# Attention with the two heads of a pair side by side in the array, splits on all partitions, one output instruction for both heads

## The chip, the core and the metric

The program runs on one core of a Trainium2 chip. TensorE (PE) multiplies matrices and writes PSUM; its weight loads have a row of their own in the profile (PEld). VectorE (DVE), ScalarE (ACT) and GpSimd (POOL) do the elementwise work, and SyncE (SP) issues the DMAs. Each engine takes its own instructions in the order in which they stand, and semaphores hold the engines together. The metric is the device time of one execution in microseconds (us).

## The reference, cut to what matters

```python
def _attn_ref(q, k, v):                       # (4, 8, 576, 64) each, float32
    q_rot, k_rot = (rotate(q), rotate(k))     # x * cos + (halves swapped, signed) * sin
    scores = (1 / np.sqrt(64)) * np.matmul(q_rot, k_rot.transpose(0, 1, 3, 2))
    attn = np.exp(scores - np.max(scores, axis=-1, keepdims=True))
    attn = attn / (np.sum(attn, axis=-1, keepdims=True) + 1e-09)
    return np.matmul(attn, v)
# the heads joined: x (4, 576, 512); then
# xk, xr: x mixed with x one token earlier, by mu_k and mu_r
# k = relu(xk @ w_k);  x = sigmoid(xr @ w_r) * (k * k @ w_v)
# u = x + token mix (576 -> 256 -> 576);  out = u + relu(u @ w_ch1) @ w_ch2
```

## The kernel before

The 32 heads are taken as 16 pairs, A and B. A pair's scores are worked on in nine tiles of 128 query rows (`TILES`, line 29): A0 to A3, B0 to B3, and R, which holds the last 64 rows of A and of B. To keep float32 accuracy every factor is split into a high part and the rest. After the rotation (`rope`, on POOL), `split_hi` (ACT) and `split_lo` (DVE for q, POOL for k) work on one head at a time, so on 64 partitions: `kst` holds a head's k with the high part on its own 64 partitions and the rest on the other 64, and `qst` holds q with the high part on all 128 and then the rest on all 128, for which a DMA copies it across (line 307). A tile of scores is then 4 matmuls over 128 partitions (2 splits of q by 2 halves of 288 keys; R takes 8), `emit_S`, line 384, into one of two buffers of PSUM (`S_p`).

Of each tile DVE takes the row maximum (`emit_max`), ACT the exponential with its sum (`emit_exp`), DVE the factor 1/sum (`emit_den`, `emit_rc`), ACT the high half of p in float16 (`emit_hi`), DVE the low half (`emit_lo`), and a DMA transposes both (`emit_tr`). A pair's output is made in four units, one head and 256 or 320 queries each (`emit_pv`, line 457): 9 matmuls of a 128-column stationary operand that holds the high and the low half of that head's v side by side. The two halves of the result are added by an ACT copy (line 465) and a DVE instruction (line 474) on 64 partitions.

`a_step` is one tile's turn, and `prep` places what the next pair needs. During the first 4 pairs the weights of the next layer are converted on DVE (`Conv`, line 163). From pair 4 on, `a_step` also draws from `kvr_gen`: the matmuls with w_k (`kp`, line 628) and w_v (`vp`, line 646) of the batches whose attention is done. These are plain float32, and the chip runs each as two instructions. `PRI` sets priorities and a scheduler makes the fixed order of each engine from them; the w_k and w_v work has the lowest one. `v_row` (line 318, a one-column stationary operand) and `v_all` (line 339, a one-row one) make the scale of v. After the attention come the weights of the later layers, the last w_k tasks and the two mixing layers, which the change does not touch.

Of the kernel before, what the change touches and what calls it, by code (L numbers as in the profile page):

```python
# [18 lines left out]
NP = H // 2  # L19
# [18 lines left out]
BUFS = dict(raw=6, vr=2, v16=2, e=7, p16=3, pt0=1, pt1=2, tm=2, sm=4, sc=3, la=1, lf=1, xs=4, xk=6, t=2, q=2, vt=2, wd=3)  # L38
# [25 lines left out]
def body(tc, qk, vw, tabs, ident, mu, w_k, w_v, w_r, w_t1, w_t2, w_c1, w_c2, out):  # L64
# [41 lines left out]
    with ctx:  # L106
# [130 lines left out]
        raw_p = right("raw", BUFS["raw"])  # L237
        tab_p = right("tab", 1)
        st_p = right("st", 1)
# [4 lines left out]
        pt0_p = right("pt0", BUFS["pt0"])  # L244
        pt1_p = right("pt1", BUFS["pt1"])
        tm_p = right("tm", BUFS["tm"])
# [3 lines left out]
        tab = tab_p.tile([128, 2, S], F32, name="tab")  # L250

        raw_t, v_t, v16_t, sc_t = {}, {}, {}, {}

        kst = [st_p.tile([128, S], F32R, name=f"kst{x}") for x in range(2)]
        qst = [st_p.tile([128, 2, QW], F32R, name=f"qst{x}") for x in range(2)]
        NG = B * NP

        @prio("ld")
        def ld_raw(g, ab=((0, 1), (1, 1), (0, 0), (1, 0))):
            if g >= NG:  # L260
                return
            for j, k in ab:
                t = raw_p.tile([128, S], F32, tag="raw", name="raw")
                sp.dma_start(t, qk[g // NP, g % NP, :, j, k])
                raw_t.setdefault(g, [[None] * 2 for _ in range(2)])[j][k] = t
# [9 lines left out]
        @prio("rope")  # L275
        def rope(g, j, k, e):
            t = raw_t[g][j]
            if k < 2:
                o = tt(e, t[k], t[k], tab[:, k], ALU.mult)
# [68 lines left out]
        @prio("v16")  # L348
        def v_hi(g):
            t = v16_p.tile([128, 9, 4, 64], F16, tag="v16", name="v16")  # L350
            v16_t[g] = t
            copy("A", v_t[g], v_t[g], sc_t[g][:, 0:1])
            act.activation(out=t[:, 0:5, 0::3, :], in_=v_t[g].rearrange("p c (h d) -> p c h d", h=2), func=AF.Copy)

        @prio("v16")
        def v_lo(g):
            v, t = v_t[g], v16_t[g]
            for x in range(2):
                o, hi = t[:, 0:5, 1 + x, :], t[:, 0:5, 3 * x, :]
                tt("P", o, v[:, :, 64 * x:64 * x + 64], hi, ALU.subtract)  # L360

        @prio("v16")
        def v_shift(g):
            t = v16_t[g]
# [5 lines left out]

        @prio("S")
# [624 lines left out]
```

## Time and profile before

| what | value |
|---|---|
| median of 3 runs | 1046.34 us (1046.04 to 1047.02) |
| the profiled execution | 1049.78 us, span 1048.0 us, mean granted clock 0.951 |
| busy, share of the span | PE 86%, weight loads 75%, DVE 61%, ACT 50%, POOL 36% |
| first matmul of scores of pair 0 | about 20 us |
| last matmul of scores of pair 15 | about 523 us |
| DMA over the span | 130.48 MB, of 216365 packets 175712 under 512 B |

The first two rows differ because the profiled execution is another one. The shares are means over very different stretches: until 149 us attention runs beside the conversion of weights, until 523 us beside the w_k and w_v matmuls, and after that there is no attention.

### The profile page before, as it was taken

How to read it: one execution, taken by the hardware profiler on the slowest of the kernel's cores; microseconds unless marked ns; L12 is line 12 of the kernel's file. 1: busy time of each engine (PE TensorE's matmuls, PEld its weight loads, DVE VectorE, ACT ScalarE, POOL GpSimd, SP SyncE). 2: the span in 40 equal slices, each digit the busy share in tenths (PEclk: the TensorE clock that was granted, in tenths of full speed). 3: DMA queues.
4: the chain of work that ended last, by engine and by line, in shares of the span. 5: the costliest groups of instructions: out<-in, count | busy, mean ns of one | idle time of the engine just before them, and what ended most of it. 6: DMA issues, size and time to landing. Idle time of an engine off the chain costs nothing.

```text
span 1048.0 us, 15540 instructions
## 1 busy us (share of the span) xinstructions
PE 903.7 (86%) x5488; PEld 782.1 (75%) x5488; DVE 643.4 (61%) x1283; ACT 525.4 (50%) x1114; POOL 377.3 (36%) x344
## 2 busy tenths in 40 slices
PE   2447557989889997799948899999999999999998
PEld 1335344767667776578827789899999999999997
DVE  6999999877678778878689636953323312231111
ACT  3666667767667786778656353443233112211110
POOL 6653476553355544532035513461132012201010
PEclk9986667999999999899979999999999999999999
DMA  6899989997888888987792044311020002000000
GB/s 195 217 206 229 220 194 181 176 203 167 182 166 190 190 177 161 198 185 157 133 321 98 23 137 159 134 42 28 1 91 24 23 2 75 1 24 1 24 23 23
DMA packets 216365, 130.48 MB, mean 125 GB/s; under 512 B 175712, under 2 KB 191200, under 8 KB 216160
## 3 DMA queue, kind: packets, MB, share of 16 engines
q1 hardware_dynamic: 216288, 129.50, 52.3%
q8 instruction: 43, 0.70, 0.3%
q14 instruction: 34, 0.28, 0.1%
HBM read 59.79 MB, written 14.16 MB: 71 GB/s over the span
## 4 chain that ended last, share of the span: by engine, by line
PE 45%; DVE 5%; issue 2%; DMA 2%; ACT 1%; POOL 1%; SPq 0%; DVEq 0%; POOLq 0%; ACTq 0%
PE co L574 4%; PE co L573 4%; PE c1p L573 4%; PE co L575 4%; PE c1p L574 4%; PE c1p L575 4%; PE vp L646 4%; PE kp L628 3%; DVE cv L203 2%; DVE cv L207 1%; PE rp L575 1%; PE rp L574 1%; PE rp L573 1%; PE pv L457 1%; PE S L384 1%
## 5 line engine op out<-in xcount | busy, mean ns | idle before, releaser
L384 PE MATMUL S<-kst,qst 128*128 128x288 f32 x640 | 140.4, 358 | 49.2 <-ACT e L398 37.0
L384 PEld LDWEIGHTS S<-kst,qst 128*128 128x128 f32 x640 | 108.9, 220 | 72.2 <-ACT e L398 47.7
L422 DVE SCALAR_TENSOR_TENSOR p<-e,rc,p 128x576 f16<-128x576 f32 x144 | 140.2, 988 | 29.6 <-ACT p L74 28.9
L628 PE MATMUL kp<-f,parts 128*128 128x288 f32 x512 | 139.6, 418 | 11.4 <-DVE f L561 8.7
L457 PE MATMUL pv<-pt,v 128*128 128x256 f16 (+1 forms) x576 | 102.9, 327 | 52.4 <-DMA pt<-p 42.0
L398 ACT ACTIVATE e<-S,nm 128x576 f32<-128x576 f32 x144 | 105.7, 735 | 76.6 <-DVE nm L391 75.4
L900 DVE SCALAR_TENSOR_TENSOR hs<-c1p,hs 128x288 fp32r<-128x288 f32 x96 | 43.5, 455 | 153.1 <-ACT hs L899 153.1
L103 POOL TENSOR_TENSOR raw<-raw,tab 128x576 f32<-128x576 f32 x62 | 97.7, 1586 | 107.5 <-DMA raw<-in_qk_dram 93.2
L646 PE MATMUL vp<-k,parts 128*128 128x288 f32 x512 | 131.5, 408 | 1.5 <-ACT vt L72 1.5
L74 ACT ACTIVATE p<-e,rc 128x576 f16<-128x576 f32 x144 | 108.8, 769 | 38.1 <-DMA pt<-p 18.5
L628 PEld LDWEIGHTS kp<-f,parts 128*128 128x128 f32 x512 | 95.8, 195 | 37.8 <-DVE f L561 9.5
L899 ACT ACTIVATE hs<-c1p 128x288 fp32r<-128x288 f32 x96 | 38.8, 408 | 169.6 <-PE c1p L575 166.2
L457 PEld LDWEIGHTS <-v 128*128 128x128 f16 x576 | 57.5, 109 | 85.3 <-issue 40.3
L573 PE MATMUL c1p<-uhl,parts 128*128 128x288 f32 x384 | 114.5, 299 | 3.8 <-DVE hs L900 2.9
L646 PEld LDWEIGHTS vp<-k,parts 128*128 128x128 f32 x512 | 94.7, 190 | 25.8 <-ACT vt L72 2.0
L575 PE MATMUL c1p<-uhl,parts 128*128 128x288 f32 x384 | 113.6, 297 | 0.0
L574 PE MATMUL c1p<-uhl,parts 128*128 128x288 f32 x384 | 113.6, 296 | 0.0
L575 PE MATMUL co<-hs,parts 128*128 128x288 f32 x384 | 113.1, 297 | 0.0
L574 PE MATMUL co<-hs,parts 128*128 128x288 f32 x384 | 112.6, 296 | 0.0
L391 DVE TENSOR_REDUCE nm<-S 128x1 f32<-128x576 f32 x144 | 106.1, 747 | 7.7 <-PE S L384 6.6
L573 PE MATMUL co<-hs,parts 128*128 128x288 f32 x384 | 108.7, 297 | 0.0
L103 POOL TENSOR_TENSOR uhl<-y,uhl 128x288 fp32r<-128x288 f32 x32 | 25.2, 816 | 209.3 <-ACT uhl L72 209.0
(101 smaller groups left out, 1855.0 us busy)
## 6 DMA issues: line engine op xcount, KB each, us to landing
raw<-in_qk_dram SPq DMA_DIRECT2D x64, 288.0 KB, 3.8
words<-in_w_c_dram SPq DMA_DIRECT2D x24, 512.0 KB, 7.8
qst<-qst SPq DMA_DIRECT2D x30, 288.0 KB, 3.5
vr<-in_vw_dram SPq DMA_DIRECT2D x16, 320.0 KB, 4.1
xd<-xT SPq DMA_DIRECT2D x16, 288.5 KB, 3.2
vd<-vt SPq DMA_DIRECT2D x32, 144.0 KB, 2.3
y<-vd SPq DMA_DIRECT2D x8, 576.0 KB, 5.5
out_dram<-y SPq DMA_DIRECT2D x8, 576.0 KB, 3.5
```

Source lines behind the costliest of these rows:

```text
L74: act.activation(out=o, in_=i, func=AF.Copy, scale=scale)
L103: return (pool if e == "P" else dve).tensor_tensor(o, a, b, op=op)
L384: pe.matmul(p[:, h, 0:HS], lhsT=qst[x][:, s, c:c + 128], rhs=kst[x][:, h * HS:(h + 1) * HS], start=(j == 0 and s == 0), stop=(j == len(par ...
L391: dve.tensor_reduce(out=nm, in_=S_t[i][:, :, 0:HS], op=ALU.max, axis=AX.XY, negate=True)
L398: act.activation(out=e, in_=S_t.pop(i)[:, :, 0:HS], func=AF.Exp, bias=sum_t[i][:, 0:1], accum_out=s)
L422: dve.scalar_tensor_tensor(out=t[:, S:2 * S], in0=e_t.pop(i), scalar=sum_t.pop(i)[:, 0:1], in1=t[:, 0:S], op0=ALU.mult, op1=ALU.subtract)
L457: pe.matmul(p[:, 0:n], lhsT=vt[:, j, 128 * x:128 * x + 128], rhs=t[:, j, :], start=(j == 0), stop=(j == 8))
L573: pe.matmul(p, lhsT=wh, rhs=t[:, 0], start=first, stop=False)
L574: pe.matmul(p, lhsT=wh, rhs=t[:, 1], start=False, stop=False)
L575: pe.matmul(p, lhsT=wl, rhs=t[:, 0], start=False, stop=last)
L628: pe.matmul(p[:, 0:HS], lhsT=wk[m // 4][kk][:, 128 * (m % 4):128 * (m % 4) + 128], rhs=xs[kk], start=kk == 0, stop=kk == KD - 1)
L646: pe.matmul(p[:, 0:HS], lhsT=wv[kf // 4][kf % 4][:, 128 * m:128 * m + 128], rhs=k2[kf], start=kf == 0, stop=kf == KF - 1)
```

## The change

The tables, the rotated halves and the splits now hold both heads on 128 partitions, head A on the lower 64 and head B on the upper 64; the scale 0.125 is in q's table. q is laid out with 640 columns, so that the last 64 queries of the heads stand in columns of their own with zeros beside them. A step takes 128 queries of both heads (`ND` = 5 steps a pair, the last is the old R). A tile of scores is three products over 64 partitions (high by high, high by rest, rest by high), written head by head in alternation; the step for the last queries uses all 128 partitions. The output is made in two units for both heads at once: 14 products for each head, head A's into the lower and head B's into the upper 64 partitions of one PSUM tile, and one ACT instruction puts it into `xT`. The rest of v comes from DVE now, and the DMA that copied q across is gone. `a_step` draws w_k and w_v work four or five times a step.

```diff
-TILES = ["A0", "A1", "A2", "A3", "R", "B2", "B3", "B0", "B1"]
-NT = len(TILES)
-PV_AT = {7: (0, 0), 10: (0, 1), 12: (1, 0), 13: (1, 1)}
+ND = 5
+PV_AT = {4: 0, 6: 1}
+UNIT = [(0, 256), (256, 320)]
...
-        def split_hi(g, x, j, e):
-            l = slice(64 * x, 64 * x + 64)
-            t = raw_t[g][j][0][l]
-            if j == 0:
-                copy(e, kst[x][l], t)
-            else:
-                copy(e, qst[x][l, 0, 64 * x:64 * x + S], t, 0.125)
+        def split_hi(g, j, e):
+            w = QW if j else S
+            hl = [sp_p.tile([128, w], F32R, tag=f"sp{j}{i}", name="kq") for i in range(2)]
+            spl_t.setdefault(g, [None, None])[j] = hl
+            copy(e, hl[0], raw_t[g][j][0])
         @prio("qk")
-        def split_lo(g, x, j, e="P"):
-            l, o = slice(64 * x, 64 * x + 64), slice(64 - 64 * x, 128 - 64 * x)
-            t = raw_t[g][j][0][l]
-            if j == 0:
-                tt(e, kst[x][o], t, kst[x][l].bitcast(F32), ALU.subtract)
-                return
-            c = slice(64 * x, 64 * x + S)
-            lo, hi = qst[x][l, 1, c], qst[x][l, 0, c].bitcast(F32)
-            dve.scalar_tensor_tensor(out=lo, in0=t, scalar=0.125, in1=hi, op0=ALU.mult, op1=ALU.subtract)
-            if g == 0:
-                copy("A", qst[x][o, :, c], qst[x].bitcast(F32)[l, :, c])
-            else:
-                sp.dma_start(qst[x].bitcast(F32)[o, :, c], qst[x].bitcast(F32)[l, :, c])
+        def split_lo(g, j, e):
+            hl = spl_t[g][j]
+            tt(e, hl[1], raw_t[g][j][0], hl[0].bitcast(F32), ALU.subtract)
...
-            t = v16_p.tile([128, 9, 4, 64], F16, tag="v16", name="v16")
-            v16_t[g] = t
-            copy("A", v_t[g], v_t[g], sc_t[g][:, 0:1])
-            act.activation(out=t[:, 0:5, 0::3, :], in_=v_t[g].rearrange("p c (h d) -> p c h d", h=2), func=AF.Copy)
+            hi = v16_p.tile([128, 9, 128], F16, tag="vh", name="vh")
+            lo = v16_p.tile([128, 5, 128], F16, tag="vl", name="vl")
+            v16_t[g] = hi, lo
+            act.activation(out=hi[:, 0:5], in_=v_t[g], func=AF.Copy, scale=sc_t[g][:, 0:1])
...
-            v, t = v_t[g], v16_t[g]
-            for x in range(2):
-                o, hi = t[:, 0:5, 1 + x, :], t[:, 0:5, 3 * x, :]
-                tt("P", o, v[:, :, 64 * x:64 * x + 64], hi, ALU.subtract)
+            hi, lo = v16_t[g]
+            dve.scalar_tensor_tensor(out=lo, in0=v_t[g], scalar=sc_t[g][:, 0:1], in1=hi[:, 0:5], op0=ALU.mult,
+                                     op1=ALU.subtract)
...
-        def emit_S(i):
-            n = TILES[i % NT]
-            p = S_p.tile([128, 2, 512], F32, tag="S", name="S")
-            parts = []
-            for x, nm in enumerate("AB"):
-                if n == "R":
-                    parts.append((x, 512 if x == 0 else 0))
-                elif n[0] == nm:
-                    parts.append((x, 128 * int(n[1]) + 128 * x))
-            for j, (x, c) in enumerate(parts):
-                for s in range(2):
-                    for h in range(2):
-                        pe.matmul(p[:, h, 0:HS], lhsT=qst[x][:, s, c:c + 128], rhs=kst[x][:, h * HS:(h + 1) * HS],
-                                  start=(j == 0 and s == 0), stop=(j == len(parts) - 1 and s == 1))
-            S_t[i] = p
+        def emit_S(j):
+            g, m = divmod(j, ND)
+            (kh, kl), (qh, ql) = spl_t[g]
+            w = heads(j)
+            ps = [S_p.tile([128, 2, 512], F32, tag="S", name="S") for _ in range(w)]
+            for h in range(2):
+                for n, (a, b) in enumerate(((qh, kh), (qh, kl), (ql, kh))):
+                    for x in range(w):
+                        l = slice(64 * x, 64 * x + 64) if w == 2 else slice(0, 128)
+                        pe.matmul(ps[x][:, h, 0:HS], lhsT=a[l, 128 * m:128 * m + 128],
+                                  rhs=b[l, h * HS:(h + 1) * HS], start=(n == 0), stop=(n == 2))
+            S_t[j] = ps
...
-        def emit_pv(g, x, u):
-            t = pt_t.pop((g, x, u))
-            n = 320 if u else 256
-            t0 = (256 * u) if x == 0 else (0 if u else 320)
+        def emit_pv(g, u):
+            t0, n = UNIT[u]
+            ts = [pt_t.pop((g, x, u)) for x in range(2)]
+            vh, vl = v16_t[g]
             p = pv_p.tile([128, 512], F32, tag="pv", name="pv")
-            vt = v16_t[g].rearrange("p c f d -> p c (f d)")
-            for j in range(9):
-                pe.matmul(p[:, 0:n], lhsT=vt[:, j, 128 * x:128 * x + 128], rhs=t[:, j, :], start=(j == 0),
-                          stop=(j == 8))
-            m, o = slice(64 * x, 64 * x + 64), slice(64 - 64 * x, 128 - 64 * x)
-            cell = []
+            prods = [(vh, j, j) for j in range(9)] + [(vl, j, j) for j in range(5)]
+            for i, (v, a, c) in enumerate(prods):
+                for x in range(2):
+                    l = slice(64 * x, 64 * x + 64)
+                    pe.matmul(p[l, 0:n], lhsT=v[:, a, l], rhs=ts[x][:, c, :], start=(i == 0),
+                              stop=(i == len(prods) - 1))
             @prio("low")
-            def low():
-                tm = tm_p.tile([128, 320], F32, tag="tm", name="tm")
-                act.activation(out=tm[m, 0:n], in_=p[o, 0:n], func=AF.Copy, scale=sc_t[g][o, 1:2])
-                cell.append(tm)
...
-            @prio("add")
-            def add():
+            def out():
...
-                dve.scalar_tensor_tensor(out=xT[b][m, pr, 1 + t0:1 + t0 + n], in0=p[m, 0:n], scalar=sc_t[g][m, 1:2],
-                                         in1=cell[0][m, 0:n], op0=ALU.mult, op1=ALU.add)
-                if (x, u) == (1, 1):
+                act.activation(out=xT[b][:, pr, 1 + t0:1 + t0 + n], in_=p[:, 0:n], func=AF.Copy,
+                               scale=sc_t[g][:, 1:2])
+                if u == 1:
                     sp.dma_start(xd[b][:, pr], xT[b][:, pr])
                     a_done.add(g)
-            return low, add
+            return out
...
             elif k == 0:
+                rope(g, 1, 0, "P")
+                rope(g, 1, 1, "P")
+                split_hi(g, 0, "A")
                 v_pow(g)
+            elif k == 1:
+                rope(g, 1, 2, "P")
+                split_lo(g, 0, "P")
+                v_all(g)
+                v_sc(g)
+                ld_raw(g + 1, 0, 0)
+                ld_raw(g + 1, 0, 1)
             elif k == 2:
-                v_all(g)
+                split_hi(g, 1, "A")
+                split_lo(g, 1, "D")
+                v_hi(g)
+                ld_raw(g + 1, 1, 0)
+                ld_raw(g + 1, 1, 1)
             elif k == 3:
-                v_sc(g)
-            elif k == 6:
-                v_hi(g)
-            elif k == 7:
                 v_lo(g)
                 v_shift(g)
...
+            if j < NTT:
+                emit_exp(j)
+            if j + 1 < NTT:
+                emit_S(j + 1)
+            other()
+            if j < NTT:
+                emit_den(j)
+            if j + 1 < NTT:
+                emit_max(j + 1)
+            if j < NTT:
+                emit_rc(j)
+                emit_hi(j)
+            other()
             for gg in (g, g - 1):
-                r = i - gg * NT
+                r = j - gg * ND
                 if 0 <= gg < NG and r in PV_AT:
-                    low, add = emit_pv(gg, *PV_AT[r])
-                    after.setdefault(i + 2, []).append(low)
-                    after.setdefault(i + 2, []).append(add)
-            if 0 <= i - 2 < NTT:
-                emit_lo(i - 2)
-                emit_tr(i - 2)
-            for f in after.pop(i, []):
+                    after.setdefault(j + 1, []).append(emit_pv(gg, PV_AT[r]))
+            if 0 <= j - 1 < NTT:
+                for x in range(heads(j - 1)):
+                    emit_lo(j - 1, x)
+                    emit_tr(j - 1, x)
+                    other()
+            for f in after.pop(j, []):
                 f()
-            with ahead(PRI["kv"]):
-                kv(KVN)
-            prep(g, k + NT)
+            other()
+            prep(g, k + ND)
             prep(g + 1, k)
-            prep(g + 2, k - NT)
+            prep(g + 2, k - ND)
...
-            if not cv.done() and i % 4 == 1:
+        v_max(1)
+        prep(1, -1)
+        for j in range(4 * ND):
+            a_step(j, lambda n: None)
+            if not cv.done() and j % 5 in (0, 2, 4):
                 cv.step()
         while not cv.done():
             cv.step()
...
-        for i in range(4 * NT, NTT + 7):
-            a_step(i, kv.advance)
+        for j in range(4 * ND, NTT + 4):
+            a_step(j, kv.advance)
```

The order of TensorE in pair 6 (pairs are counted from 0), where w_k and w_v matmuls (`kp`, `vp`) stand between score tiles (`S`; `kst` and `qst` are one head's splits). Before:

```order
L628 MATMUL kp<-f,parts 128x288
L384 MATMUL S<-kst_165,qst_167 128x288 x4
L628 MATMUL kp<-f,parts 128x288 x5
L384 MATMUL S<-kst_165,qst_167 128x288 x4
L628 MATMUL kp<-f,parts 128x288 x4
```

After, with buffer numbers (`kq` is a split of k or q, `S_2055` the PSUM tile of one head):

```order
L634 MATMUL vp_1904<-k2_1869,parts_1218 128x288
L376 MATMUL S_2055<-kq_1823,kq_1986 128x288
L376 MATMUL S_2055<-kq_1824,kq_1986 128x288
L376 MATMUL S_2055<-kq_1823,kq_1987 128x288
L376 MATMUL S_2055<-kq_1823,kq_1986 128x288
L376 MATMUL S_2055<-kq_1824,kq_1986 128x288
L376 MATMUL S_2055<-kq_1823,kq_1987 128x288
L634 MATMUL vp_1904<-k2_1913,parts_1219 128x288
```

Where four matmuls stood in a row, six stand, all of one head; the other head's six come after further `vp` rows.

The order of TensorE at an output unit of pair 6 (`pv`; `pt` is the transposed p of one head, `v` the split v). Before:

```order
L457 LDWEIGHTS v_2020
L457 MATMUL pv<-pt_2290,v_2020 128x320
L457 LDWEIGHTS v_2020
L457 MATMUL pv<-pt_2290,v_2020 128x320
L457 LDWEIGHTS v_2020
L457 MATMUL pv<-pt_2290,v_2020 128x320
```

After, the beginning of a unit that stands among the score tiles of pair 7, with the tiles, the small v matmul (`vps`) and the `kp` rows around it:

```order
L376 MATMUL S<-kq 128x288 x6
L453 LDWEIGHTS vh
L453 MATMUL pv<-pt_2629,vh 64x256
L310 MATMUL vps<-idn,vm 1x128
L376 MATMUL S<-kq 128x288 x6
L616 MATMUL kp<-f,parts 128x288 x4
L453 LDWEIGHTS vh
L453 MATMUL pv<-pt_2635,vh 64x256
L453 LDWEIGHTS vh
L453 MATMUL pv<-pt_2629,vh 64x256
L453 LDWEIGHTS vh
L453 MATMUL pv<-pt_2635,vh 64x256
```

The unit's matmuls now alternate between the two heads and write 64 partitions each, and other work stands between its first two.

## Rows read from the trace of the kernel before

**Rows 1.** Busy time by stretch: stretch, us, PE, PEld, DVE, ACT, POOL, clock, DMA, GB/s

```profile
0.00:20.00 20.00, 0.59 (x2) 0.09 (x2) 12.56 (x12) 5.10 (x6) 13.16 (x18) 1.00 0.61 198
20.00:149.00 129.00, 76.84 (x304) 54.19 (x305) 124.67 (x247) 82.60 (x156) 71.46 (x61) 0.78 0.93 215
149.00:177.00 28.00, 18.86 (x86) 12.83 (x86) 26.02 (x55) 19.05 (x37) 17.78 (x12) 0.74 0.88 175
177.00:523.00 346.00, 311.40 (x1635) 242.03 (x1634) 263.06 (x565) 253.94 (x529) 148.63 (x118) 0.99 0.85 176
523.00:600.00 77.00, 56.98 (x254) 44.30 (x252) 66.10 (x104) 39.31 (x82) 37.18 (x38) 0.87 0.44 153
```

**Rows 2.** Groups of TensorE, 177:523: count, busy us, mean ns, idle before, releaser

```profile
L628 PE MATMUL kp<-f,parts 128*128 128x288 f32 x372 | 98.4, 410 | 2.2 <-ACT t L635 1.6 <-DVE f L561 0.5
L646 PE MATMUL vp<-k,parts 128*128 128x288 f32 x376 | 96.9, 408 | 0.0
L384 PE MATMUL S<-kst,qst 128*128 128x288 f32 x444 | 87.1, 328 | 8.0 <-ACT e L398 7.8 <-issue 0.2
L457 PE MATMUL pv<-pt,v 128*128 128x320 f16 x207 | 35.3, 306 | 9.9 <-DMA pt<-p 7.2 <-DVE rc L410 2.5 <-issue 0.2
L457 PE MATMUL pv<-pt,v 128*128 128x256 f16 x198 | 27.6, 280 | 13.8 <-DMA pt<-p 9.4 <-DVE den L404 2.0 <-DVE xT L474 1.2
```

**Rows 3.** Chain of waits, 466:523: start us, us, what

```profile
472.44 1.00 PE pv L457 x9
...
477.65 1.57 PE S L384 x12
...
485.60 3.88 PE kp L628 x16
...
503.50 0.70 PE pv L457 x5
```

**Rows 4.** TensorE in time, 266:267.1: start us, us, what

```profile
265.80 0.71 PE L457 MATMUL pv<-pt,v 128*128 128x256 f16 x5
266.43 0.38 PE L318 MATMUL vps<-idn,vm 128*1 128x128 f32 x2
266.74 0.75 PE L646 MATMUL vp<-k,parts 128*128 128x288 f32 x2
```

**Rows 5.** Weight loads in the same place, with idle time before

```profile
266.74 0.30 PEld L646 LDWEIGHTS vp<-k,parts 128*128 128x128 f32 x2 [0.22 <-issue]
```

**Rows 6.** TensorE in time, 719:719.5, a 64-column transpose

```profile
719.03 0.38 PE L760 MATMUL trp<-idn,y 128*64 128x128 f32 x2
...
719.38 0.29 PE L573 MATMUL co<-hs,parts 128*128 128x288 f32 x1
```

**Rows 7.** Groups of VectorE, 49:149

```profile
L422 DVE SCALAR_TENSOR_TENSOR p<-e,rc,p 128x576 f16<-128x576 f32 x27 | 27.0, 1002 | 0.9 <-ACT p L74 0.9
...
L303 DVE SCALAR_TENSOR_TENSOR qst<-raw,qst 64x576 fp32r<-64x576 f32 x6 | 6.9, 1145 | 0.1
L410 DVE RECIPROCAL rc<-den 128x1 f32<-128x1 f32 x26 | 3.9, 149 | 0.1
L404 DVE TENSOR_SCALAR den<-sum 128x1 f32<-128x1 f32 x26 | 3.5, 136 | 0.4 <-ACT e L398 0.4
L474 DVE SCALAR_TENSOR_TENSOR xT<-pv,sc,tm 64x320 f32<-64x320 f32 x6 | 3.3, 547 | 0.6 <-ACT tm L465 0.5
L474 DVE SCALAR_TENSOR_TENSOR xT<-pv,sc,tm 64x256 f32<-64x256 f32 x5 | 2.4, 481 | 0.1
```

**Rows 8.** Groups of VectorE, whole span, whole-width operations of pair 0

```profile
L103 DVE TENSOR_TENSOR kst<-raw,kst 64x576 fp32r<-64x576 f32 x2 | 3.7, 1840 | 0.1
...
L103 DVE TENSOR_TENSOR raw<-raw 128x576 f32<-128x576 f32 x2 | 3.1, 1529 | 0.0
```

**Rows 9.** DMA issues of the page: count, KB each, us to landing

```profile
qst<-qst SPq DMA_DIRECT2D x30, 288.0 KB, 3.5
```

More of the change, by code (lines that the diff above doesn't have):

```diff
@@ L61, in drain, with body @@
             self.advance(1 << 30)
-def body(tc, qk, vw, tabs, ident, mu, w_k, w_v, w_r, w_t1, w_t2, w_c1, w_c2, out):
+def body(tc, kin, qin, vw, tabs, ident, mu, w_k, w_v, w_r, w_t1, w_t2, w_c1, w_c2, out):
     nc = tc.nc
@@ L243, in body, with ld_raw @@
         p16_p = right("p16", BUFS["p16"])
[L244 to L246 removed]
+        pt_p = right("pt", BUFS["pt"])
         sm_p = right("sm", BUFS["sm"])
         sc_p = right("sc", BUFS["sc"])
[L250 to L255, printed above, removed]
+        tab = tab_p.tile([128, 2 * (S + QW)], F32, name="tab")
+        TAB = [[tab[:, 0:S], tab[:, S:2 * S]], [tab[:, 2 * S:2 * S + QW], tab[:, 2 * S + QW:]]]
+        raw_t, v_t, v16_t, sc_t, spl_t = {}, {}, {}, {}, {}
         NG = B * NP
         @prio("ld")
[L259 removed]
+        def ld_raw(g, j, k):
             if g >= NG:
                 return
[L262 to L265, printed above, removed]
+            if j == 0:
+                t = rk_p.tile([128, S], F32, tag="rk", name="rk")
+                sp.dma_start(t, kin[g // NP, g % NP, :, k])
+            else:
+                t = rq_p.tile([128, QW], F32, tag="rq", name="rq")
+                sp.dma_start(t, qin[g // NP, g % NP, :, k])
+            raw_t.setdefault(g, [[None] * 2 for _ in range(2)])[j][k] = t
         @prio("ld")
@@ new lines, in emit_max, with emit_exp @@
+        @prio("max")
+        def emit_max(j):
+            nm = sm_p.tile([128, 2], F32, tag="nm", name="nm")
+            for x, p in enumerate(S_t[j]):
+                dve.tensor_reduce(out=nm[:, x:x + 1], in_=p[:, :, 0:HS], op=ALU.max, axis=AX.XY, negate=True)
+            sum_t[j] = nm
+        @prio("exp")
+        def emit_exp(j):
+            s = sm_p.tile([128, 2], F32, tag="sum", name="sum")
+            e_t[j] = []
+            for x, p in enumerate(S_t.pop(j)):
+                e = e_p.tile([128, 2, HS], F32, tag="e", name="e")
+                act.activation(out=e, in_=p[:, :, 0:HS], func=AF.Exp, bias=sum_t[j][:, x:x + 1],
+                               accum_out=s[:, x:x + 1])
+                e_t[j].append(e.rearrange("p a b -> p (a b)"))
+            sum_t[j] = s
@@ new lines, in emit_den, with emit_rc @@
+        @prio("den")
+        def emit_den(j):
+            d = sm_p.tile([128, 2], F32, tag="den", name="den")
+            w = heads(j)
+            dve.tensor_scalar(out=d[:, 0:w], in0=sum_t[j][:, 0:w], scalar1=1e-9, scalar2=1.0 / PSCALE, op0=ALU.add,
+                              op1=ALU.mult)
+            sum_t[j] = d
+        @prio("den")
+        def emit_rc(j):
+            r = sm_p.tile([128, 2], F32, tag="rc", name="rc")
+            w = heads(j)
+            dve.reciprocal(r[:, 0:w], sum_t[j][:, 0:w])
+            sum_t[j] = r
@@ L419, in emit_lo, with emit_hi @@
+        @prio("hi")
+        def emit_hi(j):
+            p16_t[j] = []
+            for x, e in enumerate(e_t[j]):
+                t = p16_p.tile([128, 2 * S], F16, tag="p16", name="p16")
+                copy("A", t[:, 0:S], e, sum_t[j][:, x:x + 1])
+                p16_t[j].append(t)
         @prio("lo")
-        def emit_lo(i):
-            t = p16_t[i]
-            dve.scalar_tensor_tensor(out=t[:, S:2 * S], in0=e_t.pop(i), scalar=sum_t.pop(i)[:, 0:1], in1=t[:, 0:S],
+        def emit_lo(j, x):
+            t = p16_t[j][x]
+            dve.scalar_tensor_tensor(out=t[:, S:2 * S], in0=e_t[j][x], scalar=sum_t[j][:, x:x + 1], in1=t[:, 0:S],
@@ new lines, in body, with a_step, other @@
+        NTT = NG * ND
+        after = {}
+        def a_step(j, kv):
+            g, k = divmod(j, ND)
+            def other():
+                with ahead(PRI["kv"]):
+                    kv(KVN)
+            if j < NTT:
[11 more added lines that the diff above has]
+            other()
@@ L693, in body @@
         sp.dma_start(mu_s, mu)
-        ld_raw(1)
+        for j in range(2):
+            for k in range(2):
+                ld_raw(1, j, k)
         pool.memset(ones, 1.0)
-        for x in range(2):
-            pool.memset(qst[x].bitcast(F32)[:, :, S - S * x:QW - S * x], 0.0)
         dve.tensor_scalar(out=om_s, in0=mu_s, scalar1=-1.0, scalar2=1.0, op0=ALU.mult, op1=ALU.add)
@@ L703, in body @@
                 rope(0, j, k, "DDDPPD"[3 * j + k])
-        for x in range(2):
-            for j in (1, 0):
-                split_hi(0, x, j, "A")
-                split_lo(0, x, j, "D")
-            if x == 0:
-                emit_S(0)
-                emit_max(0)
+        for j in range(2):
+            split_hi(0, j, "A")
+            split_lo(0, j, "D")
+        emit_S(0)
+        emit_max(0)
         v_max(0)
```

141 lines of the change are left out of this document (43 added, 98 removed).

## The prediction

> **What bounds the kernel now.** I read the stretches first, then TensorE's groups and the chain of waits in the longest of them, then single instructions. Attention lasts from 20 to 523 us, in three stretches [rows 1]. In 20:149 VectorE is busy 124.67 of 129 us, with the conversion of weights beside pairs 0 to 3; DMA stands at 0.93 and TensorE's granted clock at 0.78, so VectorE bounds it. In 149:177, pair 4, VectorE is at 26.02 of 28. In 177:523 VectorE is at 76% and TensorE at 311.40 of 346 us, at a clock of 0.99; the w_k and w_v work fills it. The 444 score matmuls there are 11 pairs of 40 [rows 2], so these are pairs 5 to 15, at 31.5 us each.
>
> How full TensorE really is there follows from its paces, since records of matmuls overlap. In the chain of waits 16 `kp` take 3.88 us, so 0.2425 each; 12 of S 1.57, so 0.131; 9 of `pv` with 256 columns 1.00, so 0.111; 5 with 320 columns 0.70, so 0.140 [rows 3]. Times the counts [rows 2]: 748 of `kp` and `vp` 181.4, S 58.2, `pv` 207 by 0.140 and 198 by 0.111, 51.0. With some 5 us for the small v matmuls that is 296 of 346 us; 50 us are stalls, of which the groups show waits for the transposed p and for the exponential [rows 2]. TensorE is the engine that sets these 346 us. After 523 VectorE has 66.10 of 77 us, and that work can't begin before attention has left its memory, so I carry a shift of 523 to the end in full.
>
> **The change, part by part.**
>
> *Scores on TensorE.* A pair had 40 matmuls and has 4 x 12 + 6 = 54. The 12 over 64 partitions would cost as 6 if both heads ran at once. The order speaks against it: in pairs 5 to 15 the six of one head stand together, then those of the other, because each waits for its own PSUM buffer, as the rows of `S_2055` show. So I count each at the 0.131 of a full one: 11 x 54 x 0.131 = 77.8 us, 19.6 more. The bounds: all 12 at once, 11 x 30 x 0.131 = 43.2 (15 less than now), or as I take it.
>
> *Output on TensorE.* 36 matmuls a pair become 56, in 28 couples of 64 columns each that stand next to each other. If the two of a couple run side by side, 11 x 14 x (0.111 + 0.140) = 38.7 us, 12.3 less; if one after the other 77.3, 26 more. No row shows it. I take side by side, since they use different columns and different PSUM partitions and nothing in the order parts them. The `kp` and `vp` work stays: the order has 384 of them between these pairs' scores (two instructions each), which had 390. Work on TensorE is then 296 + 19.6 - 12.3 = 303.
>
> *Changes of shape.* Before, nearly every stationary operand is 128 by 128. Now S (64 rows), `pv` (64 columns) and `kp`/`vp` (full) alternate; in the order of pairs 5 to 15 I count 310 changes between the three, 220 into or out of S. What one costs is seen where the small v matmuls stand now. Five `pv` from 265.80 at 0.109 or so each end their turn at 266.35, but the one-column `vps` starts at 266.43, 0.08 later; the two `vps`, 128 columns each and by `kp`'s pace 128/288 of 0.2425, take 0.11 each, to 266.65, and the first full `vp` has its start shown at 266.74, with 0.22 us in which the weight load waits for nothing that the profile shows [rows 4, 5]. The two `vp` last 0.75 from start to end where 0.24 + 0.41 is usual [rows 2 to 4], so another 0.10 for weights that were not loaded ahead: 0.19 in all for a change to full weights. But around a 64-column transpose nothing is lost: from its start to that of the second `co` behind it are 0.35 us [rows 6], which is two transposes of 0.11 (128 columns too) and one matmul of 0.13. So a change costs between 0 and 0.19 us. For the 220 with S I take 0.19, as its operand, like those of the small v matmuls, uses a part of the array in a plain matmul: 41.8 us. For the 90 between `pv` and full work I take 0.05, near the transpose's row: 4.5. Of the 46 together I take a quarter off for changes that fall where TensorE waits anyhow (171 of the 310 have a wait in front of them, most of them long met), leaving 35. The bounds are 0 and 310 x 0.19 = 59.
>
> The Trainium skill bears on this place. Its page "TensorEngine Tiling (Array Packing)", section Key Properties, says that changing the tiling mode, not just the tile, drains TensorE. The small v matmuls agree, with 0.08 us going in and 0.19 coming out; the 64-column transpose does not. By that rule for all changes the term would be 59 before the quarter comes off, 44 after, so 9 more than I take. The page "TensorE: Matmul & The Clock Gate", section Part 3: Packing small matmuls, gives 2.38 times for three column tiles side by side; an estimate for two from it is 2 x 2.38/3 = 1.6 times, by which the output would take 48 us and not 38.7. No run here shows that.
>
> *Stalls.* 50 us now. The w_k and w_v work is spread more evenly in the new order (20 to 38 matmuls a pair until pair 14, before 6 to 44), and the engines that feed TensorE have less to do, so TensorE will more often be the late one: I take 28, between 10 and 50. Pairs 5 to 15: 303 + 35 + 28 = 366, against 346: **+20**.
>
> *VectorE, 20:149.* Per pair [rows 7]: the four additions go, 2 x (0.547 + 0.481) = 2.06; the factors are made 5 times and not 9, 4 x (0.136 + 0.149) = 1.14; two q rests of 1.145, 2.29, become one of 128x640. Its nearest rows are 1.529 and 1.840 for 576 columns [rows 8], so 1.70 to 2.04; I take 1.9. The rest of v comes from POOL: by the p row, 1.002 x 640/576 = 1.11. Sum -2.48 a pair, -9.9 for four. Next late are DMA at 0.93 and TensorE, which at half clock would need 54 x 0.262 + 28 x 0.25 = 21 us and its changes of a pair's 32. I take **-7**, between -10 and 0. Pair 4 gives **-2** in the same way.
>
> *ACT, POOL, DMA.* ACT loses two half-width splits, a v copy and two output copies a pair, POOL half of its k rests and all of v's, the queue of SP 30 copies of 288 KB [rows 9]. In 177:523 ACT is at 73%, POOL at 43% and DMA at 0.85 [rows 1], all under TensorE, so this I cost at nothing; were TensorE not the bound it would be worth up to the 50 us of stalls.
>
> *Start.* S of pair 0 now needs q's own tables and both heads' splits: 640 KB of tables and 64 KB of q more, at 198 GB/s [rows 1] 3.6 us, partly behind VectorE. I take **+2**, between 0 and 4.
>
> **Sum.** -7 - 2 + 20 + 2 = +13 on the profiled execution's 1049.8, so 1062.8. The median of the runs is 3.4 lower: 1059.
>
> **The rivals.**
>
> *The relief shows and the changes are free.* If a change of shape costs nothing or always falls into a stall, pairs 5 to 15 take 303 + 28 = 331, -15: -22 in all, 1024; with a few us of changes left, 1028. For it: the transpose's row. Against it: the rows of the small v matmuls, in plain matmuls like these. It decides from a mean cost of 0.09 us down: there pairs 5 to 15 take 303 + 28 + 0.75 x 310 x 0.09 = 352, and the +6 cancels against the -7 of the other terms.
>
> *Both heads' scores at once.* The Trainium skill's page on tiling, section Theoretical Speedup, gives up to 2 times for a contraction of 64. Here that means S at 43.2 us and not 77.8: 1059 - 35 = 1024. Against it: only single matmuls at the seam of the two sixes stand beside one of the other head.
>
> *The output's couples run one after the other.* 38.7 us more work; the stalls would shrink to some 15, so +26: 1085.
>
> *The terms cancel.* Changes at about 0.1 us for all 310, a quarter off, 23, so pairs 5 to 15 at 354, +8, with -9 before: within 2 us of 1046.
>
> **How the numbers follow.** Forecast 0.50, relief 0.26, scores at once 0.03, couples in turn 0.12, cancelling 0.09. The forecast's own range is 1049 to 1080 (changes 20 to 44, stalls 20 to 35). With the relief at 1024 to 1028 and most of the couples' case at 1085 the range is 1022 to 1090. A difference under 0.2%, 2.1 us, is no change here. Faster: 0.26 + 0.03 + 0.03 of the cancelling = 0.32. Same: 0.05. Slower: 0.50 + 0.12 + 0.01 = 0.63.
>
> **What would show it.** S of 864 instructions at 0.13 us inside a head's six; the two `pv` of a couple starting within some ns of each other; idle time of the weight load before the first S, `pv` or `kp` behind another shape with no releaser shown, near 0.2 us; pairs 5 to 15 longer than 346 us, pairs 0 to 3 shorter than 129; no `tm`, no `qst` copies, POOL and ACT less busy. I am wrong if the weight loads run through the changes without a gap, if the two heads' sixes overlap, or if TensorE in pairs 5 to 15 still has 50 us of stalls.

## The result and the profile after

The changed kernel takes 1059.32 us (median of 9 runs, 1051.3 to 1061.43), the kernel before 1046.34 (9 runs): ratio 1.0109, 95% interval 1.008 to 1.0138, so slower by 13 us. The profiled execution of after took 1059.56 us, its span is 1057.8.

The stretches after, cut like [rows 1] but at the new bounds of the pairs (stretch, us, busy us of each engine with instructions, granted clock, DMA share, GB/s):

```profile
...
20.00:158.00 138.00, 86.53 (x413) 63.62 (x414) 130.41 (x209) 71.19 (x138) 71.35 (x58) 0.69 0.87 199
158.00:186.00 28.00, 21.38 (x135) 15.99 (x136) 24.19 (x40) 18.65 (x37) 14.51 (x10) 0.70 0.80 169
186.00:537.00 351.00, 351.00 (x1936) 248.12 (x1935) 233.73 (x430) 222.67 (x472) 111.10 (x83) 0.97 0.72 149
537.00:614.00 77.00, 69.84 (x353) 55.47 (x352) 55.77 (x93) 39.26 (x88) 33.55 (x37) 0.96 0.47 153
```

In the long stretch TensorE now shows 351.00 of 351 us: no stall is left to see. VectorE is the busiest engine of pairs 0 to 3 as before (130.41 of 138 us), but they are longer, not shorter. From the starts of the score matmuls, by 16ths of their count:

| kernel | median us | pair 5 starts | pairs 5 to 15 | rest | w_k, w_v matmuls before the last score | changes of shape in pairs 5 to 15 |
|---|---|---|---|---|---|---|
| before | 1046.3 | 177.6 | 345.2 | 525.1 | 760 | 38 |
| after | 1059.3 | 185.6 | 351.4 | 520.7 | 726 | 316 |
| den per head | 1053.9 | 178.9 | 349.5 | 525.4 | 698 | 303 |
| one tile for both heads' scores | 1132.3 | 223.5 | 381.3 | 529.8 | 780 | 165 |
| output head by head | 1054.3 | 181.4 | 343.0 | 526.1 | 696 | 217 |
| before, 64-row scores | 1065.3 | 178.8 | 356.2 | 524.5 | 736 | 170 |
| scores of full shape | 1035.5 | 181.4 | 334.1 | 518.5 | 714 | 251 |
| all of full shape | 1046.2 | 180.8 | 324.3 | 537.1 | 646 | 38 |
| den per head, q padded | 1042.1 | 175.4 | 336.8 | 521.7 | 734 | 189 |
| den and output per head | 1044.2 | 180.1 | 335.1 | 524.0 | 688 | 199 |
| output first | 1052.2 | 181.1 | 343.2 | 525.6 | 758 | 204 |
| den, padded q, output first | 1031.6 | 177.6 | 334.6 | 520.6 | 736 | 105 |

The changes are counted in the order of the instructions. The stages are of one profiled execution each, which lies up to 6 us off the kernel's median. The sixth column matters to the fourth: where TensorE is the late one, w_k and w_v work that it has not done by the last score stays for the rest.

TensorE's groups after, to set beside [rows 2] (count, busy us, mean ns, idle before):

```profile
L376 PE MATMUL S<-kq 64*128 64x288 f32 (+1 forms) x593 | 107.5, 318 | 0.0
L616 PE MATMUL kp<-f,parts 128*128 128x288 f32 x368 | 101.4, 419 | 0.0
...
L453 PE MATMUL pv<-pt,vh 128*64 128x256 f16 (+1 forms) x385 | 47.7, 310 | 0.0
...
```

The waits for p and for the exponential in [rows 2] are gone. What fills the time instead shows in the weight loads. In the long stretch of before (177:523) their idle time with no releaser (`issue`) was 1.1 us on S and 0.4 each on `kp` and `vp`:

```profile
L628 PEld LDWEIGHTS kp<-f,parts 128*128 128x128 f32 x372 | 68.0, 190 | 20.3 <-ACT t L635 3.0 <-DVE f L561 0.8 <-issue 0.4
L384 PEld LDWEIGHTS S<-kst,qst 128*128 128x128 f32 x442 | 66.3, 192 | 19.2 <-ACT e L398 12.8 <-issue 1.1 <-ACT p L74 0.2
```

In that of after (186:537) it is 16.4 and 5.3 each:

```profile
L376 PEld LDWEIGHTS S<-kq 64*128 64x128 f32 (+1 forms) x592 | 79.2, 187 | 30.5 <-issue 16.4 <-ACT p L76 2.3 <-ACT t L623 1.7
L616 PEld LDWEIGHTS kp<-f,parts 128*128 128x128 f32 x368 | 66.5, 190 | 22.5 <-issue 5.3 <-ACT vh L345 0.7 <-ACT t L623 0.5
...
```

One change in time, TensorE of after (start us, us from first start to last end):

```profile
474.80 4.63 PE L634 MATMUL vp<-k,parts 128*128 128x288 f32 x18
479.36 1.05 PE L376 MATMUL S<-kq 64*128 64x288 f32 x6
480.34 0.75 PE L634 MATMUL vp<-k,parts 128*128 128x288 f32 x2
```

Read it by starts, since the ends overlap. 18 `vp` at 0.2425 [rows 3] are 4.365 us, but S begins 4.56 later: 0.195 lost. Six S at 0.131 are 0.786, but `vp` begins 0.98 later: 0.194 lost. That is the 0.19 of [rows 4, 5], once per change, in either direction. Its weight loads show the places:

```profile
474.80 4.18 PEld L634 LDWEIGHTS vp<-k,parts 128*128 128x128 f32 x18 [0.17 <-issue]
479.36 0.82 PEld L376 LDWEIGHTS S<-kq 64*128 64x128 f32 x6 [0.39 <-issue]
```

The Trainium skill's rule that changing the tiling mode drains TensorE ("TensorEngine Tiling (Array Packing)", Key Properties) agrees with these rows.

The granted clock is the other thing that changed. Pair 12 (403:444) has the lowest of the long stretch:

```profile
403.00:444.00 41.00, 41.00 (x200) 27.59 (x200) 18.93 (x37) 19.24 (x40) 10.67 (x10) 0.83 0.51 111
```

In pairs 5 to 15 of after TensorE stands 20.5 us at half clock (1.2 GHz, 0.50 in the trace), in four stretches, and `vp` starts there every 480 ns and not every 243; in before it is 10.2 us. Each of the four begins where, with no wait, 64-row S and 64-column `pv` follow one another, mostly with one to three matmuls of each: the last comes at 423.2, and from 420.55 on one S stands between every one or two `pv`.

VectorE after, 49.8:158, against [rows 7] (count, busy us, mean ns):

```profile
...
L402 DVE TENSOR_SCALAR den<-sum 128x2 f32<-128x2 f32 x13 | 8.8, 674 | 1.7 <-ACT e L393 1.7
...
L350 DVE SCALAR_TENSOR_TENSOR vl<-vr,sc,vh 128x640 f16<-128x640 f32 x3 | 4.9, 1636 | 0.0
...
L105 DVE TENSOR_TENSOR kq<-rq,kq 128x640 fp32r<-128x640 f32 x3 | 2.4, 808 | 0.0
```

`den` of two elements a partition takes 674 ns where `den` of one took 136. Why is seen in time, VectorE first, then POOL:

```profile
87.68 1.37 DVE L402 TENSOR_SCALAR den<-sum 128x2 f32<-128x2 f32 x1
```

```profile
87.31 1.71 POOL L105 TENSOR_TENSOR kq<-rk,kq 128x576 fp32r<-128x576 f32 x1 [1.62 <-ACT kq L74]
```

POOL ends at 89.02, `den` 0.03 later. All 17 `den` of over 400 ns in the span end 23 to 29 ns after the end of a POOL instruction that runs beside them.

### The profile page after: what moved, and what is told of

Its sections match the earlier page's. It is cut to its first block, busy times and chain, and to the rows that moved or that the text cites. A ratio compares the mean times of both kernels' runs of the same rounds, so it can differ in the third digit from the quotient of the medians.

```text
span 1057.8 us, 16122 instructions
## 1 busy us (share of the span) xinstructions
PE 965.6 (91%) x6032; PEld 808.9 (76%) x6032; DVE 604.6 (57%) x1090; ACT 476.2 (45%) x1032; POOL 328.5 (31%) x295
## 4 chain that ended last, share of the span: by engine, by line
PE 72%; DVE 7%; DMA 3%; issue 2%; ACT 1%; POOL 0%; SPq 0%; DVEq 0%; ACTq 0%; POOLq 0%
PE vp L634 11%; PE kp L616 11%; PE S L376 10%; PE pv L453 6%; PE co L561 4%; PE co L562 4%; PE co L563 4%; PE c1p L561 4%; PE c1p L562 4%; PE c1p L563 4%; DVE cv L205 2%; PE rp L561 1%; PE rp L562 1%; PE rp L563 1%; DVE cv L201 1%
## 5 line engine op out<-in xcount | busy, mean ns | idle before, releaser
L376 PE MATMUL S<-kq 64*128 64x288 f32 (+1 forms) x864 | 173.8, 349 | 51.1 <-ACT e L393 47.9
L376 PEld LDWEIGHTS S<-kq 64*128 64x128 f32 (+1 forms) x864 | 133.0, 215 | 94.7 <-ACT e L393 56.8
L616 PE MATMUL kp<-f,parts 128*128 128x288 f32 x512 | 143.3, 423 | 3.4 <-DVE f L549 3.4
L634 PE MATMUL vp<-k,parts 128*128 128x288 f32 x512 | 140.7, 425 | 2.5 <-ACT vt L74 2.4
L76 ACT ACTIVATE p<-e,rc 128x576 f16<-128x576 f32 x144 | 104.2, 767 | 32.3 <-issue 11.2
L453 PE MATMUL pv<-pt,vh 128*64 128x256 f16 (+1 forms) x576 | 75.9, 346 | 8.9 <-DMA pt<-p 7.8
L561 PEld LDWEIGHTS c1p<-uhl,parts 128*128 128x128 f32 x384 | 72.2, 188 | 6.7 <-DVE hs L887 4.5
L105 POOL TENSOR_TENSOR rq<-rq,tab 128x640 f32<-128x640 f32 x32 | 59.2, 1852 | 44.6 <-DMA rq<-in_qin_dram 43.4
```

What stands on the lines that cost most here:

```text
L76: act.activation(out=o, in_=i, func=AF.Copy, scale=scale)
L105: return (pool if e == "P" else dve).tensor_tensor(o, a, b, op=op)
L376: pe.matmul(ps[x][:, h, 0:HS], lhsT=a[l, 128 * m:128 * m + 128], rhs=b[l, h * HS:(h + 1) * HS], start=(n == 0), stop=(n == 2))
L453: pe.matmul(p[l, 0:n], lhsT=v[:, a, l], rhs=ts[x][:, c, :], start=(i == 0), stop=(i == len(prods) - 1))
L561: pe.matmul(p, lhsT=wh, rhs=t[:, 0], start=first, stop=False)
L616: pe.matmul(p[:, 0:HS], lhsT=wk[m // 4][kk][:, 128 * (m % 4):128 * (m % 4) + 128], rhs=xs[kk], start=kk == 0, stop=kk == KD - 1)
```

## The experiments

Each was run against the kernel before on the same chip, in three rounds. Ratios are to the kernel before.

**1. One `den` per head.**

```
-            dve.tensor_scalar(out=d[:, 0:w], in0=sum_t[j][:, 0:w], ...
+            for x in range(w):
+                dve.tensor_scalar(out=d[:, x:x + 1], in0=sum_t[j][:, x:x + 1], ...
```

> The changed kernel with the 128x2 instruction that prepares the factor 1/sum (den) split into two of 128x1. Theory: a 128x2 den ends some 25 ns after a GpSimd operation that ran beside it and lasts up to 1.5 us, a 128x1 den lasts 0.14 us; so the mean of den falls from 0.40 to 0.14-0.16 us, pairs 0 to 4 (169.7 us in the changed kernel) become 4 to 8 us shorter, the total 1051 to 1056 us. Rival, that pairs 0 to 4 are long because TensorE stands at half clock with six score matmuls a tile: den gets short, but pairs 0 to 4 and the total change by less than 2 us.

1053.88 us, ratio 1.0069 (1.0042 to 1.0096), 5.4 less than after. The two intervals overlap, so the medians alone don't show the gain; the trace does, and so does experiment 8, which is experiment 3 with this edit, 10.1 us faster. In 49.8:155:

```profile
L403 DVE TENSOR_SCALAR den<-sum 128x1 f32<-128x1 f32 x28 | 3.8, 141 | 0.2
```

Twice as many instructions take less than half the time, and pair 5 starts 6.7 us earlier. The Trainium skill, "SBUF — State Buffer", section "SBUF: two separate sides", says that GpSimd and a VectorE operation in a two-port mode lock a shared port pair for a whole instruction. The ends of `den` right behind those of POOL agree with such a lock; that the two-element `den` is an operation in that mode, no run shows. `rc` of 128x2, at 153 ns, doesn't wait.

**2. One PSUM tile for both heads' scores**, with the twelve matmuls of the two heads in turn, so that neighbours use different halves of the rows.

```
-            ps = [S_p.tile([128, 2, 512], ...) for _ in range(w)]
+            both = S_p.tile([128, 2, 2, 512], ...)      # pool with bufs=1, was 2
+            ps = [both[:, x] for x in range(w)]
```

> The changed kernel with one PSUM tile of four banks for both heads' scores, not two tiles of two banks, so that the twelve score matmuls of a step stand alternating in the order (484 of 528 neighbours in pairs 5 to 15 are of different heads, 14 before) and there are 165 changes of shape there and not 316. Theory, that TensorE's work and changes bound pairs 5 to 15: the two heads' matmuls start within some ns of each other, S work falls from 78 to 43 us, the changes by 150 x 0.15 = 23 us, stalls of 10 to 30 us come back; pairs 5 to 15 take 300 to 330 us and not 351, the total 1010 to 1040. Rival, that the single buffer makes S wait for both exponentials: TensorE stands waiting for the time it saves, pairs 5 to 15 stay within 10 us of 351 and pairs 0 to 4 get 5 us or more longer, the total 1050 to 1075.

1132.28 us, ratio 1.0824 (1.0798 to 1.0851): far outside all that was expected. The two heads' matmuls do run side by side here: in pairs 5 to 15, at full clock, 215 S start within 20 ns of the one before, and the next couple follows some 130 ns later, the time that one S takes alone. But a single buffer lets the next scores begin only when both heads' exponentials have read it, and TensorE has stalls again (waits of TensorE in 224:605):

```profile
PE pv L454 <- DMA pt<-p: 25.7, 13, 4.9
PE kp L617 <- DVE f L550: 20.9, 5, 6.8
PE S L377 <- ACT e L394: 15.8, 8, 3.2
```

The granted clock fell too, to 0.89 in pairs 5 to 15. So the packing works, but the run doesn't show what it would gain: how the loss divides between the buffer and the clock stays open.

**3. Output head by head**: the same 56 matmuls of 64 columns, but 28 of one head and then 28 of the other.

```
-            for i, (v, a, c) in enumerate(prods):
-                for x in range(2):
+            for x in range(2):
+                for i, (v, a, c) in enumerate(prods):
```

> The changed kernel with the 28 output matmuls of a unit written head by head, not alternating. Theory, that the two of a couple run side by side in the changed kernel: the output's work in pairs 5 to 15 doubles from 38 to 77 us, some 100 changes of shape fewer give 10 to 15 back, so these pairs take 20 to 40 us more than 351 and the total is 1075 to 1100. Rival, that the starts a few ns apart are only how the trace shows queued matmuls: these pairs and the total change by less than 5 us, or fall by the changes saved.

1054.31 us, ratio 1.0083 (1.0059 to 1.0107): no slower than after (5 us less, within the spread of after's runs), where 16 to 41 more were expected. The couples of after do run side by side (starts 3 to 5 ns apart, a couple every 106 or 133 ns), and here a matmul takes 109 or 136 alone, though the scheduler left 71 of the 603 recorded ones beside one of the other head. By starts, in pairs 5 to 15, the output inside its blocks takes 32.0 us in after and 60.2 here, 28 more. Against that stand 99 fewer changes of shape (17 us at the 0.17 found below), 30 fewer `kp` and `vp` (7.3 us), and the half clock, 20.5 us of these pairs in after and none here (some 10 us). That is 34 less, and the pairs are 8.4 us shorter. Pairs 5 to 15 here, at a granted clock of 1.00 for 0.97:

```profile
181.00:525.00 344.00, 342.99 (x1921) 257.44 (x1920) 234.12 (x432) 223.74 (x472) 111.41 (x83) 1.00 0.74 153
```

**4. The kernel before with scores over 64 rows.**

```
-    lhsT=qst[x][:, s, c:c + 128], rhs=kst[x][:, h * HS:(h + 1) * HS]
+    lhsT=qst[x][l, s, c:c + 128], rhs=kst[x][l, h * HS:(h + 1) * HS]   # l: head x's 64 rows; R as before
```

> The kernel before with the score matmuls of the tiles A0 to A3 and B0 to B3 over one head's 64 partitions and not 128; count, columns and everything else stay. It leaves out the products with the rest of k, half of the contraction. Only the shape of the operand differs, which adds 132 changes of shape in pairs 5 to 15. Theory, that a change costs 0.09 us of waiting and up to 0.10 us of weight load: 12 to 25 us more TensorE time where it has 40 us of stalls, so the total is 6 to 20 us longer, and idle time with no releaser stands before the weight loads at each change. Rival, that 64 rows change nothing in plain matmuls: the total within 3 us of 1046 and no such idle time.

1065.31 us, ratio 1.0184 (1.0154 to 1.0214): nothing of the change but the shape of the scores makes the old kernel 19 us slower. The weight loads of S now show 10.5 us idle with no releaser, where they had 1.1. In pairs 5 to 15, 11.0 us longer in the profiled execution, 132 more changes are some 21 us at the 0.16 that they show here, and the waits of over 0.3 us at full clock shrink from 31.5 to 13.7. But the granted clock is 0.93 there: TensorE stands 50.5 us at half clock, where it had 10.2, and four of the five falls come behind waits of 1.6 to 3.0 us. So in this trace the changes and the clock act together, and their shares stay open. The clock alone it is not: one of the four executions had 0.947 over its span, as before has (0.937 to 0.954), and took 1064.40 us, between the others at 0.928 and 0.929 (1061.29 to 1067.34).

**5. Scores of full shape in the changed kernel.**

```
-    l = slice(64 * x, 64 * x + 64) if w == 2 else slice(0, 128)
+    l = slice(0, 128)
```

> The changed kernel with its 768 score matmuls of 64 rows over all 128 partitions (this leaves out the parting of the heads: each product holds both). Same count, same order, only the shape of S goes. Changes of shape in pairs 5 to 15 by the order: 251, where the changed kernel has 316. Theory (a change costs 0.11 to 0.19 us): pairs 5 to 15 fall from 351.4 by 7 to 12 to some 340 to 344, total 1046 to 1053. Rival (the extra time of the changed kernel there is the throttled clock and not the changes): S over all rows runs at 0.13 as before, pairs 5 to 15 stay at 349 to 353, total 1057 to 1061.

1035.51 us, ratio 0.9898 (0.9877 to 0.9919): 24 us less than after, more than the theory's 6 to 13. The same count of score matmuls takes the same pace, and what goes is idle time of the weight loads (181:516):

```profile
L376 PEld LDWEIGHTS S<-kq 128*128 128x128 f32 x594 | 88.4, 188 | 18.0 <-issue 1.4 <-ACT e L393 1.0 <-ACT p L76 1.0
```

16.4 us on S became 1.4. Pairs 5 to 15 are 17.3 us shorter: 65 fewer changes are 11 at 0.17. The granted clock is 1.00 here, so the half clock of after, some 10 us, is gone as well, although S and `pv` alternate just as in after: only S is of full shape. The rival had said that these pairs would stay as they are, and that falls, but the clock in it was a part of the cost. Pair 5 starts 4.2 us earlier, which has no explanation here.

**6. All of full shape**: experiment 5, and output matmuls over all 128 columns.

```
-    l = slice(64 * x, 64 * x + 64)
-    pe.matmul(p[l, 0:n], lhsT=v[:, a, l], ...
+    pe.matmul(p[:, 0:n], lhsT=v[:, a, :], ...
```

> The changed kernel with scores over all 128 partitions and output matmuls over all 128 columns (this leaves out the parting of the heads in both): no change of shape is left but those of the small v matmuls, 38 in pairs 5 to 15 where the changed kernel has 316. The output's work doubles, as in the version with output head by head: 324 us of work by paces, where the changed kernel has 290. Theory (a change costs about 0.09 us and more): with 38 changes pairs 5 to 15 take 324 + 3 + 3 to 15 of stalls, 330 to 342, less than the 343.0 of output head by head with its 217 changes, total 1038 to 1050. Rival (output head by head was faster by the clock alone, and changes cost nothing): pairs 5 to 15 at 343 to 346 again, total 1053 to 1056.

1046.2 us, ratio 1.0003 (0.9985 to 1.0022). Pairs 5 to 15 take 324.3 us with the doubled output, less than expected, but 114 fewer w_k and w_v matmuls than before are done by the last score, and the rest is 12 us longer than before. Against experiment 5 the couples save 10.7 us: side by side pays once the scores cost no changes.

**7. `den` per head and q padded**: experiment 1, with q of each head over 128 partitions, zeros in the other head's rows, written once; the six score matmuls of each half of the keys are also written head by head.

```
+    for x, l, c in Q_PARTS:      # head 0: rows 0:64, head 1: rows 64:128, columns 0:512; then 512:640, all rows
+        copy(e, hl[x][0][l, c], raw_t[g][1][0][l, c])
...
+    pe.matmul(ps[x][:, h, 0:HS], lhsT=a[:, 128 * m:128 * m + 128], rhs=b[:, h * HS:(h + 1) * HS], ...
```

> The changed kernel with one den instruction per head, and q stored for each head over 128 partitions with zeros in the other head's rows, so that all scores are matmuls of full shape (the same 54 a pair); the output stays in couples. ACT and VectorE make the halves of q in three instructions and not one. Changes of shape in pairs 5 to 15: 189 where the version with den per head alone has 303. Theory: 114 changes by 0.13 to 0.19 us are 15 to 22 us less in pairs 5 to 15 (349.5 to some 330), about 4 us more in pairs 0 to 4 for the longer q work; total 1036 to 1044. Rival (the changes aren't it): 1054 to 1060.

1042.09 us, ratio 0.9959 (0.9939 to 0.9979). Inside what the theory gave: 11.8 less than experiment 1, and pairs 5 to 15 in the profiled executions are 12.7 shorter though 36 more `kp` and `vp` (8.7 us) are done by the last score. The whole is faster than before. 114 fewer changes are 19 us at 0.17; the granted clock there went from 0.96 to 1.00, so some of the gain is the clock. (Its profiled execution, 1035.93 us, was its quickest, so its line in the table is some us short.)

**8. `den` per head and output head by head**: the edits of experiments 1 and 3 together.

> The changed kernel with one den instruction per head and the output head by head. Theory (the two are independent: the wait of den on pairs 0 to 4, the changes of shape and the clock on pairs 5 to 15): 1054.3 - 5.4 = 1049, between 1044 and 1051. Rival (both take away the same slack in pairs 0 to 4, where output head by head also gained 4.6 us): 1052 to 1056.

1044.18 us, ratio 0.9986 (0.9971 to 1.0001). 9.7 less than experiment 1 and 10.1 less than experiment 3, so neither edit took the other's gain. Output head by head gives more here than in experiment 3, but experiment 1 stands 27 us of pairs 5 to 15 at half clock and this run none, so not all of it is the order.

**9. Output first**: the changed kernel with the same instructions and `pv=200` for `pv=20` in `PRI`, so that blocks of couples are parted less often.

```
-PRI = dict(den=50, hi=400, pv=20, ...
+PRI = dict(den=50, hi=400, pv=200, ...
```

> The changed kernel with the same instructions in another order: the output matmuls get more priority (PRI pv=200, was 20), so that the 28 couples of a pair are less often parted by scores and w_k work. Changes of shape in pairs 5 to 15 by the order: 204, where the changed kernel has 316. Theory (the changes themselves cost 0.11 to 0.19 us): 112 fewer are 12 to 21 us less, total 1038 to 1047. Rival (the scores now come later behind a block of couples, and what feeds on them waits; or the changes are not what costs): 1055 to 1065.

1052.2 us, ratio 1.0063 (1.0042 to 1.0083). 7 less than after, where 12 to 21 were expected. Pairs 5 to 15 are 8.2 us shorter and have 32 more `kp` and `vp` (7.8 us) in them: 16 us for 112 changes, 0.14 each. That is net of 6.7 us of waits of over 0.3 us at full clock, of which after had none.

**10. `den` per head, q padded, output first**: the edits of experiments 7 and 9 together.

> The version with den per head and q padded with zeros, with the same priority for the output matmuls (PRI pv=200). Changes of shape in pairs 5 to 15: 105, where that version has 189. Theory: 84 changes by 0.11 to 0.15 us are 9 to 13 us less than its 1042, so 1029 to 1033. Rival (TensorE is so little late there that the scores' delay behind a block of couples takes it back): 1040 to 1048.

1031.56 us, ratio 0.9866 (0.9834 to 0.9898): 13.5 less than before on the same chip, the best of all. A piece of it in time:

```profile
303.59 4.04 PE L631 MATMUL kp<-f,parts 128*128 128x288 f32 x16
307.25 1.98 PE L390 MATMUL S<-kq,qp 128*128 128x288 f32 x12
309.07 2.10 PE L631 MATMUL kp<-f,parts 128*128 128x288 f32 x8
```

16 `kp` and 12 S take 5.48 us by starts; by the paces of [rows 3] they are 5.45. Between works of one shape nothing is lost.

## Why the prediction came out as it did

The time was right, 1059, but by terms that were wrong in both directions, so the hit is in good part luck. In the profiled executions the span grew by 9.8 us: 8.0 until pair 5, 6.2 in pairs 5 to 15, 4.4 less in the rest. The prediction had -7, +20 and 0. The forecast's own range, 1049 to 1080, doesn't follow from its terms either: 20 to 44 for changes and 20 to 35 for stalls give 1036 to 1075.

*Changes of shape.* The mechanism was right, and so was 0.19 us for a change with S. The 0.05 for those of the output was not: a 64-column `pv` behind `kp` costs like the others. Going in, its start is 336 ns behind that of the last `kp` for 243; coming out of 256 columns, the `kp` starts 202 to 215 ns after the last `pv` for 106, and the next `kp` 347 after it for 243. The row of the 64-column transpose [rows 6] was the wrong neighbour.

What all changes cost, and what the clock, can be told apart from the starts of TensorE in pairs 5 to 15. Take the paces off the time from start to start (0.2425 for `kp` and `vp`, 0.131 for S, half of 0.106 or 0.133 for a `pv` of a couple, 0.06 and 0.108 for the small v matmuls), and look at the full clock alone. What is left at a change and in the interval behind it is 52.3 us for 304 changes in after, 0.17 each. In experiments 4, 5, 7, 9 and 10 it is 0.16 to 0.17 each, for 102 to 251 changes. The stretches of after at half clock, with the other changes, hold 11.8 us beyond the paces. With 289 us of work that makes 353, for 351.4 measured. So the term of 35 was some 54. The quarter taken off was right in kind at most: few changes fell into a wait, as there was hardly a wait left.

*Stalls.* 28 were forecast, between 10 and 50; gaps of over 300 ns beyond the pace sum to 3.3 us, all of them at half clock, for some 40 before. Once TensorE lost some 64 us to changes and the clock, it was late everywhere; in experiment 4 too, whose edit adds nothing but changes, the waits shrink. The two terms aren't independent, and I had priced them as if they were: their errors cancelled.

*Work on TensorE.* 303 were forecast and 289 found. The scores are one after the other inside a head, at 131 to 133 ns, and the couples side by side, as forecast; had the order put the two heads' scores in turn, they would have run side by side too, as experiment 2 shows. But 34 fewer `kp` and `vp` were done by the last score, 8.2 us; "the `kp` and `vp` work stays" held for the order, not for the chip.

*VectorE in pairs 0 to 4.* Forecast -9, found +8 with the start. The step that failed is the price of `den`: I costed its halved count from the 136 ns of [rows 7] and forgot that its two elements make it another kind of operation, one that waits for POOL. Experiment 1 gives back 6.7 of the 8.0. The rest of v was dearer than 1.11 (1.64), the rest of q cheaper than 1.9 (0.81).

*Start.* Forecast +2; S of pair 0 comes 4.2 us earlier, but pair 1 begins at 49.8 us for 49.7. Neither reached the end.

*The rest.* I carried the shift in full; the rest was 4.4 us shorter, though more matmuls were left for it. No run was made on that, so it stays open.

*The clock* was no term at all. It was granted at 0.97 in pairs 5 to 15 (0.99 before), 0.93 in experiment 4, 0.96 in experiment 1, but 1.00 in experiments 3, 5, 6, 7 and 8. In after the half clock cost some 10 us there, by the 11.8 above less 11 changes. The traces show what stood before it fell in these pairs: in after all four times, and in experiment 1 six times of seven, 64-row S and 64-column `pv` in alternation without a wait; in experiments 5 and 7, where S and `pv` alternate too but S is of full shape, it never fell. In before and in experiment 4 it fell mostly behind waits of TensorE (1.2 to 3.2 us). So in after the low clock came with the mixed shapes as well. This is one trace for each kernel, and no run was made on the clock alone.

## What to carry to other kernels

Price a change of the array's shape at its two neighbours in the order, not at the instruction: packing the output of two heads side by side saved 28 us inside its blocks, which 99 more changes, 17 us, and a lower clock beside them, some 10, took back; zeros in the unused rows kept one shape, for the same number of matmuls, and won. Before folding two tiny VectorE operations into one, find a row of the wider form beside a busy POOL: here one of two elements took 674 ns where one of one element took 136. And where an engine has stalls beside it, its new costs and the stalls are one term: the new costs fill the stalls first.

## Not expected of the hardware

- `tensor_scalar` on VectorE of 128x2 fp32 ends with a POOL instruction that runs beside it and then lasts up to 1.55 us; of 128x1 it doesn't wait (131 to 157 ns, the 144 of experiment 1).
- A 64-column fp16 matmul between fp32 matmuls of full shape costs its change (336 for 243 ns behind `kp`), a 64-column transpose [rows 6] doesn't.
- A change of shape cost 0.16 to 0.17 us at full clock in six kernels whose changes in pairs 5 to 15 number 105 to 316.
